# Batch 2's cast, turns and batch 3's load placed behind the copy and fold of batch 1's low rows

## The chip, the cores and the metric

The kernel runs on one core of one Trainium2 chip. Its time is device microseconds (us) of one execution. Profiled executions give a span (first to last instruction) and a trace with every instruction's start and length; all "us" positions in this document are counted from the start of the span.

A core has five engines that each work through their own list of instructions in order: TensorE (PE in the profile, its weight loads PEld), VectorE (DVE), ScalarE (ACT), GpSimd (POOL) and SyncE (SP), which here issues DMAs only. They wait for each other through semaphores.

## The reference

Two stages follow each other. The first is an attention between a sequence and a small state, in both directions; the second adds the real part of a two-dimensional Fourier transform, normalises, and applies a two-layer network.

```python
# x: (8, 8, 512, 64)  state: (8, 8, 32, 64)      (batch, head, rows, d)
a  = softmax(x @ state.T / sqrt(64));  xread = a @ state
a2 = softmax(state @ x.T / sqrt(64));  sread = a2 @ x
x  = concat([xread, sread], rows)              # (8, 544, 512) after the heads are joined
u  = x + real(fft(fft(x, axis=rows), axis=cols))
un = (u - mean(u)) / sqrt(var(u) + 1e-6)
out = u + relu(un @ w_ch1) @ w_ch2             # 512 -> 2048 -> 512
```

## The kernel before

The eight batches go through the same stages one after another, and the stages of neighbouring batches are laid between each other so that TensorE always has matmuls to do. Per batch b they are:

- **Load and cast.** `load_x(b)` issues eight DMAs (L129) that bring x[b] into a float32 buffer `xs` (two buffers in turn). `cast_x(b)` (L132) casts it to bfloat16 in `xin` (two buffers in turn, by the parity of b). For all but part of batch 0 the cast is one GpSimd instruction.
- **Turns.** The attention needs x and the state transposed (`xT`, `sT`). Batches 0 and 1 are transposed on TensorE. From batch 2 on, `turned[b]` issues six transposing DMAs on SP: two for the state (L361), which read the blocks that GpSimd wrote into `stb` (L157), and four for x (L372), which read `xin`.
- **Scores and reads.** `attend(b)` returns two lists of steps. The first makes the scores (L405, L416) and their exponentials. The second reads the values: `read_low` computes the reversed rows 384 and on (matmuls xrp at L441, VectorE's L449 and L450 into `XR`) and copies the first 32 partitions of it into `XT` on GpSimd (L492). Those 32 are the "low rows". `sread` computes the state's reads (L460) and writes them over the same 32 partitions of `XR`: four pieces on VectorE (L469) and four on ScalarE (L471) for batch 1. `fold_low` adds and subtracts mirrored columns of `XT` on GpSimd (L495 to L497). Two more reads (xfp, L441) give `XF`. Each of these reads uses the one PSUM buffer of the pool `psX`, so the next matmul pair waits until L450 has emptied it. The folds follow: `fold_rows` (L508) of one half on GpSimd and one on VectorE, then VectorE's L522 to L535.
- **Transform.** `transform(b)` multiplies with tables of sines and cosines (L611, L565, L566), adds x (L570), takes means and variances (L321, L323), and transposes the result into `unT`.
- **Network.** `layer1(b)` (L730; for batch 0 in quarters, L740, emptied by ScalarE's L742) and `layer2(b)` (L794, emptied by VectorE's L761), then the stores, most of them issued by SP.

The weights are loaded by DMAs that GpSimd issues: w1 at L292, w2 in `last_loads` at L309. `last_loads` first waits on GpSimd for the first piece of batch 2's x (L307).

No scheduler moves anything: every engine's instructions stand in the order in which the steps are called. The change touches the list at L833 to L837, which is written out by hand for the stretch between the transform of batch 0 (`t0`), the attention of batch 1 (`s1` for its scores, `r1` for its reads: `r1[0]` is `read_low`, `r1[1]` `sread`, `r1[2]` `fold_low`, `r1[3]` and `r1[5]` the xfp reads, `r1[4]` GpSimd's fold, `r1[7]` the last read and the rest of the fold), and layer 1 of batch 0 (`L`). Here `turned[2]` and `load_x3` (the states of batches 3 to 7 and the x of batch 3) stand early in the list, right after `last_loads`, which ends with `cast_x(2)`.

Of the kernel before, what the change touches and what calls it, by code (L numbers as in the profile page):

```python
# [30 lines left out]
def kernel(  # L31
# [72 lines left out]
    def load_state(lo, hi, src=state):  # L104
        nc.sync.dma_start(
            out=stf[:, lo:hi].rearrange("p b g d -> p (b g) d"),
            in_=src[lo:hi].rearrange("b (g hh) j d -> (hh j) (b g) d", hh=4),
        )
# [4 lines left out]
    def load_x(b):  # L113
        xs = wk.tile([128, 4 * dm], F32, name="xs", tag="xs")
        xs_of[b] = xs
        v = xs.rearrange("p (i h d) -> p i h d", i=4, d=D)
        xb = x[b].rearrange("h s d -> s h d")
        for ps, si, rows in (
            (slice(0, 128), 0, xb[1:129]),
            (slice(0, 128), 1, xb[144:272]),  # L120
            (slice(0, 128), 2, xb[273:401]),
            (slice(32, 128), 3, xb[416:512]),
            (slice(0, 15), 3, xb[129:144]),
            (slice(16, 31), 3, xb[401:416]),
            (slice(15, 16), 3, xb[0:1]),
            (slice(31, 32), 3, xb[272:273]),
        ):
            queue = nc.scalar if b == 0 and si in (0, 2) else nc.sync
            queue.dma_start(out=v[ps, si], in_=rows)  # L129

    def cast_x(b, copy=nc.gpsimd.tensor_copy, lo=0, hi=4):
        copy(xin_bufs[b % 2][:, lo:hi, 1:513], xs_of[b].rearrange("p (i c) -> p i c", i=4)[:, lo:hi])  # L132
# [21 lines left out]
    def state_blocks(lo, hi, copy=nc.scalar.copy):  # L154
        for hh in range(4):
            pq = slice(32 * hh, 32 * hh + 32)
            copy(stb[pq, lo:hi, :, 4 + 64 * hh:68 + 64 * hh], stf[pq, lo:hi, :, :])  # L157

    def state_ones(lo, hi):
        for hh in range(4):  # L160
            pq = slice(32 * hh, 32 * hh + 32)
            nc.vector.memset(stb[pq, lo:hi, :, hh:hh + 1], 1.0)
            nc.vector.memset(stb[pq, lo:hi, :, 260 + hh:261 + hh], 1.0)
# [142 lines left out]
    def last_loads():  # L306
        nc.gpsimd.tensor_copy(gate[:, 0:1], xs_of[2][:, 0:1])  # L307
        for q in range(4):
            nc.gpsimd.dma_start(out=w2[:, q * 4:(q + 1) * 4, :], in_=w2v[:, q * 4:(q + 1) * 4, :])  # L309
        state_blocks(2, 3, nc.gpsimd.tensor_copy)  # L310
        cast_x(2)

    def qt(name, dt=F32):
        return psQ.tile([128, 512 if dt == F32 else 1024], dt, name=name, tag="q")
# [27 lines left out]
    turned = {}  # L342
# [375 lines left out]
    def layer1(key):  # L718
        low = isinstance(key, tuple)
        n = 128 if low else 512  # L720
        hT = wk.tile([128, FC, n], BF16, name="hTL" if low else "hT", tag="hTL" if low else "hT", bufs=1 if low else 2)
        h_of[key] = hT
        per = 512 // n

        def step(i):
            ph = psF.tile([128, 512], F32, name="ph", tag="c")
            for f in range(per * i, per * i + per):
                o = (f % per) * n
                for c in range(DC):
                    nc.tensor.matmul(ph[:, o:o + n], lhsT=w1[:, c, f * 128:(f + 1) * 128], rhs=un_of[key][:, c, :],  # L730
                                     start=(c == 0), stop=(c == DC - 1))
            nc.scalar.activation(hT[:, per * i:per * i + per, :].rearrange("p a b -> p (a b)"), ph, AF.Relu,  # L732
                                 scale=-1.0 if key in flipped else 1.0)

        def quarter_step(i, r):
            ph = psF.tile([128, 512], F32, name="ph", tag="c")
            for f in range(4 * i, 4 * i + 4):
                o = 128 * (f % 4)
                for c in range(DC):
                    nc.tensor.matmul(ph[:, o:o + 128], lhsT=w1[:, c, f * 128:(f + 1) * 128],  # L740
                                     rhs=un_of[key][:, c, 128 * r:128 * r + 128], start=(c == 0), stop=(c == DC - 1))
            nc.scalar.activation(hT[:, 4 * i:4 * i + 4, 128 * r:128 * r + 128], ph.rearrange("p (a b) -> p a b", b=128),  # L742
                                 AF.Relu, scale=-1.0 if key in flipped else 1.0)

        if key == 0:
            return [lambda i=i, r=r: quarter_step(i, r) for r in range(4) for i in range(FC // 4)]
        return [lambda i=i: step(i) for i in range(FC // per)]
# [63 lines left out]
    def warm(n):  # L811
        t = psF.tile([128, 512], F32, name="warm", tag="c")
        for i in range(n):
            nc.tensor.matmul(t[:, 0:128], lhsT=ident, rhs=ident, start=(i == 0), stop=(i == n - 1))  # L814

    def warmed(steps, n):
        return [lambda s=s: (s(), warm(n)) for s in steps if s is not None]
# [4 lines left out]
    t0 = transform(0)  # L822
# [5 lines left out]
    load_x3 = lambda: (load_state(3, B, s_dram), load_x(3))  # L828
    scores_next, reads_after = attend(2)
    L, M, r1, t1 = layer1(0), layer2(0), reads_next, transform(1)  # L830
    W = lambda n: (lambda: warm(n))
    turns1, copies1, s1 = s1[0], s1[1:4], s1[4:]
    for step in (warmed(t0[:2], 2) + [alternate, more_loads] + warmed(t0[2:4], 2) + [exp_again, last_loads, turned[2], load_x3,  # L833
            t0[4], t0[8], W(6), turns1, t0[5], W(10), t0[7], copies1[0], copies1[1], t0[6], copies1[2],
            L[0], s1[0], t0[9], L[1], t0[10], s1[1], L[2], t0[11], t0[12], L[3], s1[2], r1[0], L[4], s1[3],
            r1[2], t0[13], L[5], r1[1], L[6], r1[3], L[7], r1[4], r1[5], L[8], r1[7],
            lambda: state_ones(2, B), lambda: [r() for r in first_roots], L[9], L[10]]):  # L837
        step()
    weave((L[11:], 0, 0.25), (t1, 0.2, 1), ([M[i] for i in (0, 4, 1, 5, 2, 6, 3, 7, 8, 9)], 0.33, 0.99),
# [51 lines left out]
```

The softmax here doesn't subtract the row's maximum and nothing guards it: scores larger than these inputs give would overflow.

## Time and profile before

| what | value |
|---|---|
| median of six executions | 308.74 us (305.61 to 310.77) |
| the profiled execution's own time | 306.19 us |
| its span | 304.4 us |
| TensorE's mean granted clock | 0.993 |
| busy: PE / DVE / ACT / POOL | 290.0 / 179.8 / 139.3 / 96.4 us |
| longest wait of TensorE after 39 us | 1.5 us, for VectorE's L450 |

A line of the timeline has the start in us, the length in us, the engine, the source line, the operation, the output and its inputs, the shapes and the number of instructions merged in it. In brackets stands the time for which the engine had been idle, with what ended it. A line of the chain of waits has a start, a length, and the engine or DMA with the line. A line of the list of waits has who waited, for whom, the total, how often and the longest.

### The profile page before, as it was taken

Reading aid. Unit: us, or ns where it says so; the run is one execution under the profiler, and the core shown is the slowest. Engines: PE = TensorE matmul, PEld = TensorE weight load, DVE = VectorE, ACT = ScalarE, POOL = GpSimd, SP = SyncE. Lnnn points to the kernel's source line nnn. Section 1 sums busy time; section 2 is a strip of 40 time slices with the busy share of each in tenths; the row PEclk is TensorE's granted clock in tenths of the full one; section 3 lists DMA queues with packets and bytes.
Section 4 is the critical chain, followed back from the end, with each engine's and each line's share of the span. In section 5 each row is a group of like instructions: output and inputs, shape, how many; then the busy total and the mean of one; then the engine's idle time right before and its main releaser. Section 6 shows DMA issues by size and latency. Waiting matters only on the chain.

```text
span 304.4 us, 6017 instructions
## 1 busy us (share of the span) xinstructions
PE 290.0 (95%) x2295; PEld 168.2 (55%) x2326; DVE 179.8 (59%) x433; ACT 139.3 (46%) x267; POOL 96.4 (32%) x217
## 2 busy tenths in 40 slices
PE   5978979999999999999999999999999999999996
PEld 4767978545544555456544554445444544555443
DVE  7785765958688395773827665674668474100012
ACT  5767856666543553335443445245523442333300
POOL 4887575391263033500406022701240031000000
PEclk9989999999999999999999999999999999999999
DMA  7997999143742943446352784263333023600345
GB/s 161 220 196 175 176 172 202 40 105 69 191 104 56 221 110 101 98 105 140 111 127 64 131 181 88 76 130 72 86 88 70 37 69 86 131 9 34 71 131 145
DMA packets 110906, 34.86 MB, mean 115 GB/s; under 512 B 102062, under 2 KB 106414, under 8 KB 110878
## 3 DMA queue, kind: packets, MB, share of 16 engines
q1 hardware_dynamic: 100158, 28.72, 42.9%
q0 software_dynamic: 4224, 4.19, 8.5%
q10 hardware_dynamic: 6496, 1.57, 2.3%
q8 instruction: 18, 0.29, 0.4%
q14 instruction: 10, 0.08, 0.1%
HBM read 22.41 MB, written 14.02 MB: 120 GB/s over the span
## 4 chain that ended last, share of the span: by engine, by line
PE 82%; DMA 6%; SPq 5%; DVE 3%; POOL 2%; issue 1%; ACT 0%; POOLq 0%; DVEq 0%; ACTq 0%
PE po L794 36%; PE ph L730 34%; SPq L129 5%; DMA s_dram<-in_state_dram 4%; PE gp L611 3%; PE ph L740 2%; DMA xs<-in_x_dram 2%; POOL xin L132 1%; PE po L786 1%; PE xfp L441 1%; PE yp L566 1%; PE yp L565 1%; PE xrp L441 1%; PE eTp L428 1%; DVE U L570 1%
## 5 line engine op out<-in xcount | busy, mean ns | idle before, releaser
L794 PE MATMUL po<-w,hT 128*128 128x512 bf16 x478 | 121.6, 379 | 1.5 <-issue 0.6
L732 ACT ACTIVATE hT<-ph 128x512 bf16<-128x512 f32 x112 | 66.8, 597 | 118.2 <-PE ph L730 116.1
L730 PE MATMUL ph<-unT,w 128*128 128x512 bf16 x435 | 112.7, 379 | 0.6
L730 PEld LDWEIGHTS <-w 128*128 128x128 bf16 x576 | 50.6, 98 | 47.1
L794 PEld LDWEIGHTS <-hT 128*128 128x128 bf16 x496 | 46.9, 98 | 46.5
L761 DVE SCALAR_TENSOR_TENSOR ot<-po,rstd,U 128x512 f32<-128x512 f32 (+2 forms) x33 | 24.2, 734 | 51.1 <-PE po L794 46.3
L570 DVE TENSOR_TENSOR U<-yp,XR 128x512 f32<-128x512 f32 x16 | 10.9, 684 | 26.0 <-PE yp L566 26.0
L615 POOL COPY GL<-G 128x128 bf16<-128x128 bf16 x8 | 2.3, 291 | 75.4 <-ACT G L612 75.4
L327 POOL TENSOR_TENSOR rstd<-mv,epst 128x1 f32<-128x1 f32 x34 | 7.5, 221 | 47.3 <-DVE mv L323 47.3
L328 POOL TENSOR_TENSOR rstd<-rstd,mhalf 128x1 f32<-128x1 f32 x34 | 21.2, 624 | 2.7
L321 DVE BATCH_NORM_STATS2 st<-U 128x6 f32<-128x512 f32 x32 | 21.8, 682 | 0.1
L612 ACT CAST G<-gp 128x288 bf16<-128x288 f32 x31 | 14.6, 485 | 8.2 <-PE gp L611 8.2
L740 PE MATMUL ph<-unT,w 128*128 128x128 bf16 x256 | 16.1, 219 | 0.5 <-ACT unT L651 0.5
L132 POOL CAST xin<-xs 128x2048 bf16<-128x2048 f32 (+1 forms) x9 | 14.5, 1611 | 6.2 <-DMA xs<-in_x_dram 3.2
L814 PE MATMUL warm<-ident 128*128 128x128 bf16 x144 | 12.5, 236 | 3.7 <-POOL ident masks.py:199 3.6
L740 PEld LDWEIGHTS <-w 128*128 128x128 bf16 x256 | 15.0, 98 | 0.8 <-issue 0.6
L639 DVE TENSOR_SCALAR ub<-U,mv 128x512 bf16<-128x512 f32 x24 | 12.3, 513 | 0.9
L814 PEld LDWEIGHTS <-ident 128*128 128x128 bf16 x144 | 10.3, 107 | 4.1 <-POOL ident masks.py:199 3.6
L492 POOL COPY XT<-XR 32x514 bf16<-32x514 bf16 x8 | 4.8, 603 | 22.0 <-DVE XR L450 21.7
L450 DVE TENSOR_TENSOR XR<-xrp,rs 128x512 bf16<-128x512 f32 x16 | 11.1, 695 | 1.0 <-POOL XR L281 0.4
L570 DVE TENSOR_TENSOR U<-yp,XF 128x510 f32<-128x510 f32 x16 | 10.8, 674 | 0.0
L742 ACT ACTIVATE hT<-ph 128x512 bf16<-128x512 f32 x16 | 9.3, 598 | 3.2 <-PE ph L740 3.1
(187 smaller groups left out, 370.7 us busy)
## 6 DMA issues: line engine op xcount, KB each, us to landing
xs<-in_x_dram SPq DMA_DIRECT2D x22, 256.0 KB, 4.6
w<-in_moe_w_ch_dram POOLq DMA_DIRECT2D x8, 512.0 KB, 11.2
out_dram<-ot SPq DMA_DIRECT2D x15, 256.0 KB, 3.2
r_dram<-ot SPq DMA_DIRECT2D x14, 256.0 KB
out_dram<-r_dram SPq DMA_DIRECT2D x14, 256.0 KB, 3.6
xs<-in_x_dram SPq DMA_DIRECT2D x8, 192.0 KB, 3.7
xs<-in_x_dram ACTq DMA_DIRECT2D x2, 256.0 KB
l_dram<-ot SPq DMA_DIRECT2D x2, 256.0 KB
```

Source lines behind the costliest of these rows:

```text
L129: queue.dma_start(out=v[ps, si], in_=rows)
L132: copy(xin_bufs[b % 2][:, lo:hi, 1:513], xs_of[b].rearrange("p (i c) -> p i c", i=4)[:, lo:hi])
L321: nc.vector.bn_stats(st6, u)
L328: nc.gpsimd.tensor_tensor(rstd, rstd, mhalf, op=ALU.pow)
L570: nc.vector.tensor_add(u.rearrange("p (k r) -> p k r", r=2), p.rearrange("p (r k) -> p k r", r=2)[:, 0:u.shape[1] // 2, :], x.rearrange("p ...
L612: (nc.vector.tensor_copy if b == 0 and j == 3 else nc.scalar.copy)(G[:, j, :].rearrange("p (i q) -> p q i", q=2), p[:, 0:NM].rearrange("p ...
L730: nc.tensor.matmul(ph[:, o:o + n], lhsT=w1[:, c, f * 128:(f + 1) * 128], rhs=un_of[key][:, c, :], start=(c == 0), stop=(c == DC - 1))
L732: nc.scalar.activation(hT[:, per * i:per * i + per, :].rearrange("p a b -> p (a b)"), ph, AF.Relu, scale=-1.0 if key in flipped else 1.0)
L740: nc.tensor.matmul(ph[:, o:o + 128], lhsT=w1[:, c, f * 128:(f + 1) * 128], rhs=un_of[key][:, c, 128 * r:128 * r + 128], start=(c == 0), st ...
L761: nc.vector.scalar_tensor_tensor(ot[:, cols], in0=po_of[i][:, 0:cols.stop - cols.start], scalar=rstd, in1=u[:, cols], op0=ALU.mult, op1=AL ...
L794: nc.tensor.matmul(po_of[i], lhsT=h_of[key][:, f, i * 128:(i + 1) * 128], rhs=w2[:, f, :], start=(f == 0), stop=(f == FC - 1))
L814: nc.tensor.matmul(t[:, 0:128], lhsT=ident, rhs=ident, start=(i == 0), stop=(i == n - 1))
```

## The change

In `last_loads` the call `cast_x(2)` at the end is taken out. In the list, `turned[2]` and `load_x3` are taken out of their place after `last_loads`, and one step that calls `cast_x(2)`, `turned[2]()` and `load_x3()` in this order is put behind `r1[2]`.

```diff
         state_blocks(2, 3, nc.gpsimd.tensor_copy)
-        cast_x(2)
...
-    for step in (warmed(t0[:2], 2) + [alternate, more_loads] + warmed(t0[2:4], 2) + [exp_again, last_loads, turned[2], load_x3,
+    for step in (warmed(t0[:2], 2) + [alternate, more_loads] + warmed(t0[2:4], 2) + [exp_again, last_loads,
...
-            r1[2], t0[13], L[5], r1[1], L[6], r1[3], L[7], r1[4], r1[5], L[8], r1[7],
+            r1[2], lambda: (cast_x(2), turned[2](), load_x3()), t0[13], L[5], r1[1], L[6], r1[3], L[7], r1[4], r1[5], L[8], r1[7],
```

In the engines' lists this moves one instruction on GpSimd: the cast of batch 2 (L132) stood ahead of L492, L495, L496 and L497 of batch 1 and stands behind them. SP issues the same DMAs in the same order. TensorE's, VectorE's and ScalarE's orders are the same. In the changed file every line after the removed call has a number lower by one.

## The prediction

> **What bounds the kernel now.** I read the page's busy times first, then TensorE's waits after 39 us, then the chain of waits around 30 to 43 us, then the timeline of the same stretch.
>
> ```profile
> PE 290.0 (95%) x2295; PEld 168.2 (55%) x2326; DVE 179.8 (59%) x433; ACT 139.3 (46%) x267; POOL 96.4 (32%) x217
> ```
>
> TensorE is busy for 290.0 of 304.4 us, so only the 14.4 us in which it isn't can be won. Most of that lies before 30 us and in the 3 us after the last matmul. TensorE's waits from 39 us to the end are these (line, who released it, total, times, longest):
>
> ```profile
> PE xfp L441 <- DVE XF L450: 1.5, 1, 1.5
> PE po L794 <- issue: 0.6, 4, 0.2
> PE tp L648 <- ACT ub L637: 0.3, 1, 0.3
> PE xfp L441 <- DVE XR L450: 0.2, 1, 0.2
> ```
>
> One wait of 1.5 us stands out. The chain of waits tells where it comes from (start, length, what):
>
> ```profile
> 30.55 5.70 DMA xs<-in_x_dram
> ...
> 36.58 1.89 POOL xin L132
> 38.47 0.56 POOL XT L492
> ...
> 39.05 0.27 DVE XR L469
> ...
> 40.56 0.70 DVE XF L450
> ...
> 41.31 0.41 PE xfp L441 x2
> ```
>
> The load of batch 2's x ends at 36.25; GpSimd casts it (L132), and only then copies batch 1's low rows (L492). L469 on VectorE writes over the rows that this copy reads, so it waits for the copy; L450, which empties the PSUM buffer that the second xfp matmul wants, is queued behind L469. The timeline has each engine's own view, with its idle time in brackets:
>
> ```profile
> 35.05 0.70 DVE L450 TENSOR_TENSOR XR<-xrp,rs 128x512 bf16<-128x512 f32 x1
> 36.58 1.89 POOL L132 CAST xin<-xs 128x2048 bf16<-128x2048 f32 x1 [2.98 <-DMA xs<-in_x_dram]
> 37.42 0.17 DVE L462 RECIPROCAL rcs<-srp 128x1 f32<-128x1 f32 x1 [0.91 <-PE srp L460]
> 38.41 0.60 POOL L492 COPY XT<-XR 32x514 bf16<-32x514 bf16 x1
> 38.55 0.38 PE L441 MATMUL xfp<-stb,ET 128*128 128x260 bf16 x2
> 38.78 1.06 PE L740 MATMUL ph<-unT,w 128*128 128x128 bf16 x16
> 39.05 1.17 DVE L469 TENSOR_SCALAR XR<-srp,rcs 32x64 bf16<-32x64 f32 x4 [1.47 <-POOL XT L492]
> ```
>
> The low rows were ready at 35.75 (end of L450), while GpSimd sat 2.98 us waiting for the load. VectorE was ready for L469 at 37.59 and lost 1.47 us. TensorE ran out at 39.84.
>
> [...] the copy's input was there at 35.75 and it started at 38.41, behind the cast. [...] The wait here is 1.47 us and the granted clock from 39 to 42 us is 1.00, so the stall costs its own length and nothing after it. [...] the cast at 68.05 took 1.88 us with an L450 beside it, which took 0.69 as elsewhere. [...] the last 2 KB piece of batch 2's x, issued at 30.55 behind the w2 load that GpSimd issued from 29.26, took 5.70 us.
>
> **The change part by part.** Nothing is added or removed; GpSimd's row is the same but for one L132, now behind L492, L495, L496 and L497. SP's order is unchanged.
>
> Copy and fold: L492 starts some 0.07 us after its input (at 88.16 it follows an L450 that ended at 88.09), so at 35.82; its 2.06 us with the fold (38.41 to 40.47) end at 37.88. Gain for VectorE: L469 starts at 37.60 instead of 39.05. Four L469 and the reciprocal L462 end at 38.97. L449 then needs the first xfp pair, which ends at 38.93, so it starts at 38.96 (it was 40.33); 0.19 plus 0.04 plus 0.69 of L450 gives 39.88, and xfp follows 0.06 later at 39.94 instead of 41.31: 1.37 us. TensorE's L740 before it ends at 39.84, so 0.10 us of wait is left. TensorE's own work is late next, which is why no more than 1.47 can come out of this stall.
>
> What follows xfp keeps its spacing. ScalarE's L471, behind L462, moves from 40.51 to 39.05, and the L742 queued behind it, which empty layer 1's buffers, from 41.81 to 40.35. L450, xrp, the fold on VectorE (44.14 to 49.33) and the transform's first matmul (49.22) all move by 1.37.
>
> Cast: it starts at 37.88 instead of 36.58 and ends at 39.77 (1.30 later). Behind it on GpSimd is L508, which needs ScalarE's L471 (end 40.32) anyway: it starts at 40.4 (41.86 before). Cost nothing. If the load is late, L508 has until VectorE's L522 (44.67, now 43.30) less its 1.16, so the cast may end at 42.1, 2.3 later than planned, before anything feels it.
>
> Turns of batch 2: the two of the state (L361) wait for the state's blocks alone and stay at 33.62. The four of x (L372) wait for the cast and go from 38.49 to 39.8; the last issue ends at 45.4 instead of 44.07. With 2.5 us to landing (the median of this kernel's turns) they land by 47.9; with the 7.6 us that a state turn took beside the w2 load, the last, issued at 44.05, lands at 51.7. Their reader, L416, stood at 53.37 and now stands at 52.0. So the cost is 0 at both ends, with 0.3 to 4.1 us of slack.
>
> Load of batch 3 (L105, eight L129): 44.12 to 54.62 becomes 45.4 to 55.9. SP's next work is a store that waited until 59.66 for its tile (now 58.3), and the data's first reader on GpSimd ran at 68.05. Cost 0; without that cover it would be at most the 1.3 us.
>
> Sum on the profiled execution: 306.19 (span 304.4 and 1.79 around it) − 1.37 = 304.8. From 43 us on TensorE hardly waits again, so the shift should reach the end whole.
>
> **The median.** The profiled execution lies 2.55 under the median of the six runs, 308.74, which spread over 5.2 us. No trace tells where the others lose it. If the tail of batch 2's load lands X later, the old kernel pays X in full on the chain above; the new one hides it up to 2.3 us past its own start of the cast, and 1.3 of delay is free anyway. So the gain is 1.37 if none of the 2.55 is there, and 3.9 if all is. I take a little under a third, 0.8: 308.74 − 1.37 − 0.8 = 306.6.
>
> **The rivals.** (a) *The stall goes and no more:* 307.4; with a share of the late load, down to 306. This with 306.6 is my forecast: chance 0.48. (b) *The late load is what spreads the runs:* gain 3.9, so 304.8. For it: 5.70 us for 2 KB, on the chain of every start. Against: one profile, and the weight and state loads could spread the runs as well, in both kernels. Chance 0.30. (c) *The gain is eaten:* the cast now runs from 37.88 to 39.77 beside L469 and L450. If they lock each other out, VectorE loses up to 1.89 us and the result is 308.74 + 0.5 = 309.2. Against: the pair at 68 us above. Chance 0.10. (d) *The turns come too late, slower:* L416 stands in TensorE's one queue, and everything behind it waits. The point is a landing more than 7.9 us after the issue at 44.05; each us beyond it costs one. At 11.2 us, the w loads' median, TensorE waits 3.3 us, net +1.9: 310.6; by 13 us the kernel is over 1% slower. For it: the turns' slack shrinks by 2.7 us. Against: the w2 load is past by 44 us and the state turn's 7.6 was beside its thick. Chance 0.12, half of it over 1%. That the change isn't what it says can be left out: GpSimd's order shows it.
>
> **How the numbers follow.** 1% of 308.74 is 3.1 us, about what a measurement of this kernel can tell from no change: faster means under 305.65, slower over 311.8. Faster: all of (b) and 0.08 of (a), 0.38. Slower: half of (d), and 0.03 for what I don't see, 0.09. Within 1%: 0.53. The range reaches down to (b)'s 304.8 and a little under, 304.5, and up past (c)'s 309.2 to 309.4; it leaves out most of (d) and the tail of (b).
>
> **What would show it.** In the changed kernel's profile: L492 at about 35.8 and L132 behind L497 at 37.9; no wait of VectorE's L469 for the copy; TensorE's wait for XF at 0.1 or gone; L508 on GpSimd at about 40.4; the turns of x at 39.8; L416 at about 52.0 with no wait; the first gp matmul at about 47.9. The prediction is wrong if L416 waits for a DMA, if L450 or the cast gets longer, or if the 1.37 us is there at 48 us and gone later.

## The result, and the profile after

| | before | after |
|---|---|---|
| median of all executions | 306.86 us (69) | 305.09 us (34) |
| lowest and highest | 305.14 to 312.18 us | 304.62 to 305.65 us |
| the profiled execution's own time | 306.19 us | 304.84 us |
| its span | 304.4 us | 303.1 us |
| ratio after / before | | 0.9941, 95% interval 0.9925 to 0.9957 |

The kernel is faster by 0.6%. The interval excludes 1, and the change is inside the 1% within which the prediction expected it with the largest chance. The medians differ by 1.77 us, the profiled executions by 1.35. As striking as the median is the spread: 7.0 us before, 1.0 us after. (Executions of the kernel before that lie more than 1.5% above its fastest are left out of the ratio.) The changed kernel's line numbers are one lower from L311 on.

TensorE's waits from 39 us to the end, in the changed kernel:

```profile
PE po L793 <- issue: 0.6, 4, 0.2
PE tp L647 <- ACT ub L636: 0.3, 1, 0.3
PE xfp L440 <- DVE XR L449: 0.2, 1, 0.2
```

The 1.5 us for XF is gone and nothing has come in its place. The timeline around the cast:

```profile
35.82 0.61 POOL L491 COPY XT<-XR 32x514 bf16<-32x514 bf16 x1 [1.42 <-DVE XR L449]
37.70 1.17 DVE L468 TENSOR_SCALAR XR<-srp,rcs 32x64 bf16<-32x64 f32 x4
38.23 1.89 POOL L132 CAST xin<-xs 128x2048 bf16<-128x2048 f32 x1 [0.35 <-DMA xs<-in_x_dram]
39.23 0.69 DVE L449 TENSOR_TENSOR XF<-xfp,rs 128x512 bf16<-128x512 f32 x1
39.98 0.40 PE L440 MATMUL xfp<-stb,ET 128*128 128x260 bf16 x2
40.15 3.82 SPq L371 DMA_TRANSPOSE xT<-xin  x3
40.52 1.17 POOL L507 TENSOR_TENSOR Sm<-XF,XR 128x514 bf16<-128x514 bf16 x1 [0.40 <-ACT XR L470]
```

The copy starts as soon as its input is there (35.82), VectorE's L468 has no bracket any more, and the second xfp stands at 39.98 instead of 41.31. In this execution the load of batch 2 was later than in the one before: the cast had to wait for it again and started at 38.23. By experiment 1 below, the old order would have paid for that; here TensorE didn't notice. The chain that ended last no longer holds any DMA or SP work:

```profile
PE 89%; DVE 4%; POOL 4%; ACT 2%; issue 1%; POOLq 0%; DVEq 0%; ACTq 0%
```

Before, DMAs (6%) and SP's issues (5%) were on it.

### The profile page after: what moved, and what is told of

It reads as the page before. It is cut to its first block, busy times and chain, and to the rows that moved or that the text cites. A ratio compares the mean times of both kernels' runs of the same rounds, so it can differ in the third digit from the quotient of the medians.

```text
span 303.1 us, 6017 instructions
## 1 busy us (share of the span) xinstructions
PE 289.6 (96%) x2295; PEld 168.0 (55%) x2326; DVE 180.0 (59%) x433; ACT 139.3 (46%) x267; POOL 97.2 (32%) x217
## 4 chain that ended last, share of the span: by engine, by line
PE 89%; DVE 4%; POOL 4%; ACT 2%; issue 1%; POOLq 0%; DVEq 0%; ACTq 0%
PE po L793 36%; PE ph L729 34%; PE ph L739 4%; PE gp L610 3%; PE warm L813 2%; PE po L785 1%; PE xfp L440 1%; PE xrp L440 1%; PE yp L564 1%; PE yp L565 1%; PE esp L415 1%; PE eTp L427 1%; DVE U L569 1%; PE srp L479 1%; PE eTp L404 1%
## 5 line engine op out<-in xcount | busy, mean ns | idle before, releaser
L793 PE MATMUL po<-w,hT 128*128 128x512 bf16 x478 | 121.6, 379 | 1.5 <-issue 0.6
L793 PEld LDWEIGHTS <-hT 128*128 128x128 bf16 x496 | 46.9, 98 | 46.5
L326 POOL TENSOR_TENSOR rstd<-mv,epst 128x1 f32<-128x1 f32 x34 | 8.2, 240 | 46.7 <-DVE mv L322 46.7
L132 POOL CAST xin<-xs 128x2048 bf16<-128x2048 f32 (+1 forms) x9 | 14.4, 1605 | 3.8 <-DVE gen L235 3.0
```

The costliest lines, as they stand in the source:

```text
L793: nc.tensor.matmul(po_of[i], lhsT=h_of[key][:, f, i * 128:(i + 1) * 128], rhs=w2[:, f, :], start=(f == 0), stop=(f == FC - 1))
```

## The experiments

**1. The kernel before, three more profiles.** No edit. The question is what spreads its times.

> The kernel before, unchanged, profiled again. Theory (late load): the spread of its times is the landing of batch 2's x; each profile's span is 303.1 us plus what VectorE's L469 waits for the copy of the low rows (1.3 to 1.5 us in the first profile), and that wait grows one for one with the moment at which the last piece of the load lands (36.25 us there). Rival (spread elsewhere): spans differ by more than 0.5 us while L469's wait stays at 1.5 us; the rest then stands in the start (before 30 us) or in TensorE's clock.

> As the look before: span = 303.1 us + the wait of L469 within 0.4 us by the theory; span moving without the wait by the rival.

> As the look before: span = 303.1 us + the wait of L469 within 0.4 us by the theory; span moving without the wait by the rival.

| profile of before | cast starts | wait for XF | span | own time |
|---|---|---|---|---|
| first | 36.58 | 1.47 | 304.4 | 306.19 |
| look1 | 36.31 | 1.29 | 304.1 | 305.9 |
| look2 | 38.16 | 2.69 | 306.0 | 307.76 |
| look3 | 38.48 | 3.24 | 307.6 | 309.41 |

The time goes with the landing of batch 2's load. In each look VectorE's L469 waited as long for the copy as TensorE then waited for XF (1.28, 2.69 and 3.24 us). Span minus wait is 302.9, 302.8 and 303.3 for the first three: the wait is nearly the whole difference, as the theory said. In look3 it is 304.4, outside the 0.4 us that the theory allowed: 1.1 to 1.6 us are lost a second time. Stretches of look2 and then of look3 (stretch, its length, busy us and instructions of PE, PEld, DVE, ACT and POOL, then TensorE's granted clock, the DMA share and GB/s) show where:

```profile
44.00:46.00 2.00, 1.86 (x33) 1.67 (x31) 1.44 (x4) 1.33 (x3) 2.00 (x5) 1.00 1.27 196
46.00:48.00 2.00, 2.00 (x39) 2.00 (x37) 1.86 (x4) 1.41 (x3) 1.92 (x4) 1.00 2.25 135
```

```profile
44.00:46.00 2.00, 2.00 (x20) 1.72 (x18) 1.26 (x3) 1.39 (x3) 2.00 (x4) 0.52 1.51 126
46.00:48.00 2.00, 2.00 (x25) 2.00 (x24) 1.86 (x4) 0.60 (x1) 1.92 (x4) 0.62 2.31 118
```

After look2's wait of 2.69 us the clock stays at 1.00; after look3's of 3.24 us it is 0.52 and 0.62 on average in these stretches (which fits 0.50 from 44.1 to 47.5 us), and TensorE gets 20 and 25 matmuls done in stretches that held 33 and 39. From xfp to the first gp matmul it takes 7.91 us in look2 and 9.27 in look3: 1.36 us more.

**2. The copy on VectorE, nothing moved.** The stall can be removed without touching the cast, the turns or the load of batch 3:

```diff
         def read_low():
             xread(384, True, "xrp", XR[:, 0, 1:513])
-            nc.gpsimd.tensor_copy(XT, XR[0:32, 0, :])
+            (nc.vector.tensor_copy if b == 1 else nc.gpsimd.tensor_copy)(XT, XR[0:32, 0, :])
```

> The order of before, but batch 1's copy of the low rows (L492) is done by VectorE right behind L450, so that nothing of batch 1 that L469 needs stands behind the cast. The cast, the turns and the load of batch 3 stay early. Theory (the stall is L469's wait for a copy queued behind the cast): the wait is gone, TensorE's second xfp starts at about 40.0 instead of 41.3, and the time is that of the changed kernel, 305.1 us, or up to 0.3 more where a very late load holds GpSimd's fold; turns of x at 38.5 as before. Rival (the gain comes from moving the turns and the load of batch 3 on SP): the time stays at that of before, about 306.9 us.

305.26 us (four executions, 304.26 to 305.32; ratio 0.9883, 0.9803 to 0.9962, to seven of before at 307.85). The copy took 0.29 us on VectorE at 36.09; L469 started at 37.93 without a wait, and the second xfp at 40.27. The turns stayed early (39.01, right behind a cast at 37.09). So the gain is L469's wait for the copy, and not where the turns and the load of batch 3 stand.

**3. Only the copy ahead of the cast.** The new step one place earlier, ahead of the fold:

```diff
-            r1[2], lambda: (cast_x(2), turned[2](), load_x3()), t0[13], L[5], ...
+            lambda: (cast_x(2), turned[2](), load_x3()), r1[2], t0[13], L[5], ...
```

> The changed kernel, but the cast, turns and load stand between the copy (L492) and the fold: only the copy is ahead of the cast. Theory: L469 needs the copy alone, so the time is that of the changed kernel, 305.1 us within 0.3; GpSimd's fold ends some 2 us later (about 41 us) and L508 at about 41.5 instead of 40.5, in time for VectorE at 43.3. Rival (the fold ahead of the cast is needed too): 0.5 to 1.5 us slower than the changed kernel.

305.13 us (20 executions, 304.64 to 306.41; ratio 0.9941, 0.9921 to 0.996). The fold ended and L507 (L508 of before) followed at 41.54, about 1 us later than in the changed kernel, and TensorE waited no longer for it (the same 1.1 us in all after 39 us). Of the four instructions that the change put ahead of the cast, only the copy mattered in these executions.

**4. The load late on purpose, in both kernels.** At the end of `load_x` the last 2 KB piece is loaded once more into the same part of `xs`, and so behind the first (in the trace of the old order the first landed at 37.15 us and the second took from 37.16 to 42.54):

```diff
             queue.dma_start(out=v[ps, si], in_=rows)
+        for _ in range(1 if b == 2 else 0):
+            nc.sync.dma_start(out=v[31:32, 3], in_=xb[272:273])
```

> The kernel before with the last 2 KB piece of batch 2's x loaded a second time, which must wait for the first (its landing comes 3 to 6 us later). Theory: the kernel before pays all of it: L469's wait grows by 3 to 6 us and the time to 310 to 313 us. Rival (the end is set by TensorE's other work): within 1 us of before.

> The changed kernel with the same second load of the last piece. Theory: L469 doesn't see it; GpSimd's L508 and so VectorE's L522 do once the cast starts after about 40.2 us, so of 3 to 6 us no more than 0 to 2 reach the end: 305.1 to 307 us. The turns land by 51 us and L416 doesn't wait. Rival (late turns): L416 waits for the turns, and the time goes to 308 us or more.

Before: 312.54 us (four executions, 311.19 to 314.46; ratio 1.0191, 1.0126 to 1.0255). After: 306.36 us (20, 304.68 to 310.2; ratio to the kernel before 0.9976, 0.9954 to 0.9998). The extra load costs the old order 5.7 us on its median and the new one 1.3. In the profiled execution of the old order (lines shifted by two) TensorE waited

```profile
PE xfp L443 <- DVE XF L452: 7.3, 1, 7.3
```

and the changed kernel's profile, one of its longest executions (310.2), shows the limit of what it hides:

```profile
44.99 1.89 POOL L134 CAST xin<-xs 128x2048 bf16<-128x2048 f32 x1 [6.63 <-PE ph L741]
46.84 1.15 POOL L509 TENSOR_TENSOR Sm<-XF,XR 128x514 bf16<-128x514 bf16 x1
51.49 0.24 PE L612 MATMUL gp<-TC,XQ 128*128 128x144 bf16 x1 [3.00 <-DVE XQ L526]
```

The cast came 7 us late and ended at 46.88. GpSimd's L509 (L508 of before) stands behind it, VectorE's fold behind that, and TensorE's first gp waited 3.00 us. The turns were no limit: L416's counterpart didn't wait. (The bracket's releaser, a TensorE line, had long been done; the cast's other waits are for the load.) Here too the wait cost more than its length: at the first gp the execution was 3.6 us behind the changed kernel's profile (51.49 against 47.89), at its end 5.3 (a span of 308.4 against 303.1). In the stretches behind the wait (columns as in experiment 1) the clock was

```profile
52.00:54.00 2.00, 1.78 (x10) 0.93 (x9) 1.79 (x10) 0.77 (x2) 1.84 (x4) 0.54 0.58 123
54.00:56.00 2.00, 2.00 (x13) 1.09 (x11) 0.13 (x3) 0.48 (x1) 0.89 (x3) 0.60 0.93 211
```

0.54 and 0.60 on average, which fits 0.50 from 52.2 to 55.6 us. So the clock fell behind a wait of 3.00 us as well.

**5. The turns behind the load of batch 3.** This prices the slower rival (d):

```diff
-            r1[2], lambda: (cast_x(2), turned[2](), load_x3()), ...
+            r1[2], lambda: (cast_x(2), load_x3(), turned[2]()), ...
```

> The changed kernel with SP's load of batch 3 ahead of the turns of batch 2 (they then stand behind nine more DMA issues, some 10.5 us of issue time in the profile before). Rival (d) of the prediction, priced: the turns of x are issued at about 45 to 51 us instead of 40 to 46, the last lands at 53 to 56 us, L416 waits from 52 us, and each us past 52 costs one: 306 to 309 us. If the time stays at 305.1 with the turns landing after 52 us, the price of one us for each is wrong.

311.76 us (four executions, 311.07 to 312.47; ratio 1.0165, 1.0101 to 1.0229): slower than expected. The turns of x were issued from 52.89 to 58.00 us, since the load's eight issues (L129) took 18.1 us on SP, where they had taken 9.9 in the kernel before and 7.9 in the changed one. The load's issues began at 31.67 us, 2.7 us behind the first of the w2 load (28.95). In the changed kernel's trace w2's queue was nearly through at 44 us (366 packets from 42 to 44, 72 from 44 to 46). Here two of SP's eight issues took 6.68 and 4.34 us, between 35.19 and 46.25, and the next two 0.95 and 0.67. TensorE's timeline:

```profile
55.33 0.40 PE L415 MATMUL esp<-sT,xT 128*128 128x64 bf16 x4 [2.42 <-DMA xT<-xin]
56.65 0.40 PE L415 MATMUL esp<-sT,xT 128*128 128x64 bf16 x4 [0.92 <-DMA xT<-xin]
56.86 3.60 PE L793 MATMUL po<-w,hT 128*128 128x512 bf16 x8
```

The waits sum to 3.34 us, but the span grew by 6.4 (309.5 against 303.1). 0.7 of it was there at the first gp matmul (48.60 against 47.89). The rest, 2.4 us, goes with the clock, and eight L793 took 3.60 us instead of 1.89:

```profile
54.00:56.00 2.00, 0.40 (x4) 0.24 (x4) 1.90 (x6) 0.00 (x0) 0.53 (x2) 0.79 0.61 128
58.00:60.00 2.00, 2.00 (x6) 0.76 (x5) 0.00 (x0) 0.43 (x1) 0.00 (x0) 0.50 0.32 65
```

The mean of 0.79 from 54 to 56 us fits a fall from 1.00 to 0.50 at 55.2, 2.2 us into the first wait and ahead of the second. It was 0.51 from 60 to 62 us and 1.00 from there, so it rose again at 62.0. The clock thus fell during a wait of 2.42 us here, though behind look2's of 2.69 it didn't: in these runs the length of a wait alone doesn't tell.

**6. TensorE kept busy in the wait.** In experiment 4 the old order waited 7.3 us and took 9.92 us from xfp to the first gp, with the clock at 0.50 from 46 to 52 us; look2 took 7.91 at 1.00. Is it the wait that the clock follows, and does it cost time? The old order with the same late load, and a hundred matmuls on a constant tile (`W(100)`), whose result nothing uses, ahead of the second xfp:

```diff
-            r1[2], t0[13], L[5], r1[1], L[6], r1[3], L[7], r1[4], r1[5], L[8], r1[7],
+            r1[2], t0[13], L[5], r1[1], L[6], r1[3], L[7], r1[4], W(100), r1[5], L[8], r1[7],
```

> The kernel before with the late load (as in before_load_late), and 100 matmuls of the identity with itself, 56 ns each and used by nothing, ahead of TensorE's second xfp: they fill some 5.6 us of the 7.3 us in which TensorE waited. Theory [...]: the clock stays at 1.00 after the wait, from xfp to the first gp matmul it takes 7.7 us again instead of some 9.9, and the time falls by about 2.2 us to 309.5 to 311 us, although nothing arrives earlier. Rival (the clock is a bystander): within 0.5 us of 312.5 us, or slower.

The clock came out as expected, the time didn't. In the trace the clock stayed at 1.00, where without these matmuls it was 0.50 from 46 to 52 us. From xfp to the first gp it took 8.52 us (0.76 of it a new wait for a PSUM buffer) instead of 9.92, and TensorE's last matmul ended at 307.56 instead of 309.69. But the span was 312.2 against 312.7, because the work after TensorE's last matmul took 4.6 us instead of 3.0, for a reason that isn't shown, and the time was 313.69 us (four executions, 312.73 to 314.18), not the expected 309.5 to 311 and not below the 312.54 without these matmuls. Each side has four executions, which differ among themselves by 1.5 and 3.3 us, so this doesn't weigh the two; that the clock follows this wait is shown (0.50 with it, 1.00 with it filled), a gain from filling it is not.

**7. What delays the load.** I had put the late last piece down to the w2 load, issued from 29.26 us on, 1.3 us ahead of the piece (30.55). First only a quarter of w2 was loaded. Layer 2 then takes that quarter four times, so three quarters of its weights are left out of the result:

```diff
-        for q in range(4):
+        for q in range(1):
             nc.gpsimd.dma_start(out=w2[:, q * 4:(q + 1) * 4, :], in_=w2v[:, q * 4:(q + 1) * 4, :])
...
-                nc.tensor.matmul(po_of[i], ..., rhs=w2[:, f, :],
+                nc.tensor.matmul(po_of[i], ..., rhs=w2[:, f % 4, :],
```

> The kernel before with only the first quarter of w2 loaded by GpSimd (layer 2 then uses that quarter four times: three quarters of the weights are left out, the matmuls are as many as before). Theory [...]: the last piece lands in 2 to 4 us instead of 5.7, at 33 to 35 us; the cast ends before the low rows are ready at 35.8, L469's wait goes, and the time is about 305 us with hardly any spread, with every order as before. Rival (the last pieces are late by themselves, through the eight issues of 0.4 to 1.1 us and the state's detour): they land at 36 us as before and the time stays near 306.9 us.

Not as expected: 309.84 us (20 executions, 306.33 to 311.95; ratio 1.0057, 1.0023 to 1.0091), and the cast still started at 37.29. In this run the profile puts the end of the cast's wait down to a state turn that landed at 37.09, and not to x. So I tried the other neighbour of those pieces, the state turns that SP issues right behind them, with the whole of w2 loaded again:

```diff
-                turned[b] = lambda: (turn_state(), turn_x(0), turn_x(1))
+                turned[b] = lambda: (turn_x(0), turn_x(1), turn_state()) if b == 2 else (turn_state(), turn_x(0), turn_x(1))
```

> The kernel before with batch 2's two state turns issued behind its four x turns instead of ahead of them, so that SP issues no transposing DMA while the last pieces of batch 2's x are under way. If the state turns hold up those pieces: the cast starts at 33 to 35 us, ahead of the low rows, L469's wait goes, and the time is about 305 us. If they don't: the cast starts at 36 to 38 us as before, and the time is 306 to 308 us. (The first quarter of w2 alone left the cast at 37.3 us, so I no longer expect either with confidence.)

306.7 us (20 executions, 305.25 to 312.55; ratio 0.997, 0.9936 to 1.0003), cast at 37.48, behind x's load: with the state turns out of the way it was as late. Last, no w2 at all. Layer 2 works on columns of w1, and w2 is left out of the result:

```diff
-        for q in range(4):
-            nc.gpsimd.dma_start(out=w2[:, q * 4:(q + 1) * 4, :], in_=w2v[:, q * 4:(q + 1) * 4, :])
...
-                nc.tensor.matmul(po_of[i], ..., rhs=w2[:, f, :],
+                nc.tensor.matmul(po_of[i], ..., rhs=w1[:, f % 4, 512 * (f // 4):512 * (f // 4) + 512],
```

> The kernel before without any load of w2 (layer 2 takes columns of w1 in its place: w2 is left out of the result, the matmuls are as many as before). With a quarter of w2 loaded, the queue of SP's transfers moved next to nothing for the 2.5 us in which that quarter ran. If w2 is what holds up the last pieces: without it they land within 3 us of their issue, the cast starts at 32 to 34 us, and the time is about 305 us. If not: cast at 36 us or later, 306 us or more.

305.19 us (15 executions, 304.58 to 306.07; ratio 0.994, 0.9916 to 0.9965), in the old order:

```profile
33.14 1.89 POOL L132 CAST xin<-xs 128x2048 bf16<-128x2048 f32 x1 [2.62 <-DMA xs<-in_x_dram]
36.62 0.61 POOL L490 COPY XT<-XR 32x514 bf16<-32x514 bf16 x1 [1.59 <-DVE XR L448]
```

With no w2 load beside x's, the cast is over at 35.03, before the low rows are ready, and time and spread are close to those of the changed kernel. So the w2 load is what makes the cast late. With a quarter of it the cast was late too: in that run's trace, between 32 and 34 us w2's queue moved 393 packets and SP's queue 4, and in the us after, with w2 down to 44, SP's queue moved 546. Whether x's last piece or the state turn held the cast there isn't shown. Why the median with a quarter is above that of before stays open too: its profile is of one of its fastest executions (307.08 us).

## Why the prediction was right

The forecast was 306.6 on a median of 308.74, a ratio of 0.9931, with 0.9941 measured. In microseconds: 2.1 forecast, 1.77 measured. The median of before itself came out at 306.86 once there were 69 executions.

- **Copy, fold, L469, xfp.** Right within a tenth of a us: L492 at 35.82 (35.82 forecast), L469 at 37.70 (37.60), xfp at 39.98 (39.94), first gp at 47.89 (47.9), own time 304.84 (304.8). Experiment 2 shows that the stall is L469's wait for the copy.
- **Costs put at nothing.** The cast hid behind ScalarE's L471, L508 started at 40.52 (40.4), the turns of x at 40.15 (39.8), L416 at 52.04 without a wait, SP's first store at 58.35 (58.3). L450 took 0.69 us and L469 1.17 with the cast beside them, and 0.70 and 1.17 without it in the kernel before, so rival (c), that they lock each other out, is refuted for these instructions.
- **The late load.** The forecast took 0.8 us for what the other executions of before lose through it. Looks 1 to 3, experiment 4 and the run without w2 show the mechanism, and it is rival (b)'s: the landing of the load spread the runs of before. The size of (b), 3.9 us, was tied to a median of six executions, 2.55 us above the profile. The median of 69 is 0.67 above it, and 0.42 us lie between the difference of the medians (1.77) and that of the profiles (1.35). The forecast's 0.8 was "a little under a third" of the 2.55 without a reason for the share, so it was luck that the sum came this close. The means of all executions, 307.21 and 305.10 us, differ by more, 2.11 us, since the long executions of before weigh in them.
- **The limit of the late load.** That the cast may end at 42.1 was right for VectorE, but TensorE has about 2 us more. In the kernel before, the fold's first result for gp was ready at 47.26, and the first gp matmul stood at 49.22, behind other work of TensorE:

  ```profile
  46.83 0.43 DVE L525 TENSOR_TENSOR XQ<-XE 128x256 bf16<-128x256 f32 x1
  ```

  When the cast ended at 46.88, 4.8 us past the limit, the first gp waited 3.0 us.
- **"The stall costs its own length and nothing after it."** True for the 1.47 us of the profile and still at 2.69, but not as I used it further on. Rival (d)'s price, one us for each us of lateness, was wrong: 3.34 us of waits cost 5.7 (experiment 5), with the clock at 0.50 for 6.8 us. (d) counted no cost beyond the waits themselves. The clock fell after waits of 3.24 and 3.00 us and during one of 2.42 us, and stayed at 1.00 after 2.69.
- **The w2 load as the cause of the late piece.** The prediction had one row for it, the 5.70 us of a 2 KB piece issued behind the w2 load, which was no proof. It took the run without w2 to show it: the cast started at 33.14 instead of 36.58. By what means w2 delays the piece isn't shown.

No variant tried beats the changed kernel: 305.13 and 305.26 for the other two ways of getting the copy out from behind the cast are the same within their spread. The stall is gone in all three, and from 39 us on the listed waits of TensorE sum to 1.1 us in the changed kernel.

## What to carry to other kernels

When an engine works in order, look at what stands behind an instruction that waits for a DMA: here a short copy whose input was there at 35.75 us, 0.5 us before the load's end, started at 38.41 and held up VectorE, ScalarE and TensorE, and placing it first cost nothing that these runs show. In this kernel a wait for a DMA on the chain that sets the end showed in the spread of the times (7.0 us against 1.0) even more than in the median, so a single profile may show little of its price. Before pricing a rival in which TensorE waits, compare the wait with the shortest one with which this kernel's clock was seen to drop (2.42 us here). Here waits of 2.42, 3.00 and 3.24 us went with a fall to 0.50 and cost more than themselves; one of 2.69 us didn't.

## What the runs showed of the hardware

- The granted clock stayed at 1.00 after a wait of 2.69 us (look2). Worked out from its means over 2 us, as one step each way, it fell to 0.50 at 44.1 us, 0.9 us after the end of a wait of 3.24 us (look3), where it cost 1.36 us more; at 52.2 us, 0.7 us after the end of one of 3.00 us (changed kernel, late load); and at 55.2 us, 2.2 us into one of 2.42 us (turns behind the load).
- It stayed at 0.50 for 3.4 us in the first two of these falls (44.1 to 47.5 and 52.2 to 55.6 us), and for 6.8 us in the third (55.2 to 62.0) and in the old order with the late load, where it fell 5.3 us into the wait of 7.3 us (45.6 to 52.5).
- With a hundred matmuls on a constant tile, used by nothing, the clock stayed at 1.00 (38 to 60 us) in a place where, without them, it had fallen to 0.50 during a wait of 7.3 us.
- In the kernel before, from 32 to 36 us, w2's queue moved 688 packets (0.69 MB) and SP's queue 32, while the last 2 KB piece of batch 2's x, issued at 30.55, was on its way; it landed at 36.25. How many of SP's packets were ready in that time isn't shown.
- While a quarter of w2 (0.5 MB) was moving, SP's queue moved almost nothing: 4 packets against 393 in 2 us (32 to 34 us), and 546 against 44 in the us after. Here too it isn't shown how many of SP's were ready.
- The nine DMA issues for batch 3 took 18.8 us on SP when they stood right behind batch 2's load, beside w2, and later on 10.5 us in the kernel before and 8.6 in the changed one, so the same transfers differed in issue time.
